# Talking-heads attention and a gated MLP on one core: score blocks, key transposes, mixing weights and low parts in another order

## The chip, the cores and the metric

The kernel runs on 1 core of one Trainium2 chip. The metric is the device time of one execution in microseconds, as the median of several runs. A profile of one further execution shows where the time goes. The engines are TensorE (PE in the rows, PEld for its weight loads), VectorE (DVE), ScalarE (ACT), GpSimd (POOL) and SyncE (SP), which only issues transfers.

## What is computed

Attention over 4 batches, 12 heads, 448 positions and 64 columns per head, in which the heads are mixed twice, and a two-layer MLP behind it:

```python
scores = scale * np.matmul(q, k.transpose(0, 1, 3, 2))
scores = np.einsum('bhij,hg->bgij', scores, w_pre)
scores = scores - np.max(scores, axis=-1, keepdims=True)
attn = np.exp(scores)
attn = attn / (np.sum(attn, axis=-1, keepdims=True) + 1e-09)
attn = np.einsum('bhij,hg->bgij', attn, w_post)
out = np.matmul(attn, v)
h = x @ w_in                      # x: out as 1792 x 768; w_in 768 x 2048, w_out 2048 x 768
y = (h * (1.0 / (1.0 + np.exp(-h)))) @ w_out
```

## The kernel before

The attention stage takes the first half of the span, the MLP the second. Query rows are cut into tiles of 120, 120, 120 and 100 rows for each batch; `seq` numbers these tiles n = 0 to 15. A tile is cut into groups of 10 query rows, so that it has 12, 12, 12 and 10 groups, and one pass of the loop over groups is a slot: slots 0 to 11 are tile 0, 36 to 45 tile 3 (the short one), and slot 46 begins batch 1 with tile 4. `first[n]` is the slot in which tile n begins.

For each tile, `prep_q` transposes q on TensorE (`pt`, ScalarE takes the high part `qh`, VectorE the low part `ql`), `prep_k` does the same for a pair of heads of the keys (`kh`, `kl`), once per batch. `scores` multiplies them for one pair of heads (`pqk`, six products in two PSUM banks); the even head is copied to `st` by ScalarE (L313), the odd one by VectorE (L311), and each copy is sent by SP to a tile `g` (L320), in which the rows lie as (query row, head). Head 11's rows go in two transfers of 5 partitions. `mix_pair` mixes the heads of two groups with `w_pre` (`pp`, L364), `top` takes the maxima (L370), `exp` the exponentials, `norm` the reciprocal and the scaled `w_post` (`wr`, on GpSimd), `mix_again` mixes with `w_post` (`pa`, L390), `put` evacuates it (L399), and `values` multiplies with v (`po`, L336). Beside this, `convert` turns the MLP's weights from 64-bit to 32-bit floats and writes them to DRAM: it loads `cw` and stores `wi_dram` by SP's queue and works a step per slot on VectorE, ScalarE and GpSimd.

What stands in which slot is written as a table: `put(i, what, ...)` files a step under slot i, and with `lead` a load so many slots sooner. The scores of tile n are filed in three blocks of two pairs of heads around the slots p0 = first[n - 1] of the tile before:

```python
i = p0 + ((-6, -2, 2) if n > 1 else (0, 0, 2))[h // 4]
for hg, i in ((0, p0 - 8), (1, p0 - 4)):            # prep_q, loads 4 slots sooner
for h, i, lead in zip(range(0, H, 2), (-5, -1, 3, 7, 11, 12), (4, 5, 4, 5, 5, 4)):   # keys, from c0 = first[n - 2]
```

A slot of the loop runs in this order: loads, `mix_pair` for the pair of groups LEAD = 4 slots ahead (even slots only), evacuations that earlier slots left, `top` of the fresh pair, the low parts and odd score copies that earlier slots left (VectorE), `norm`, `exp`, the steps filed for this slot, `mix_again`, a step of `convert`. The four banks of `ps_m` serve `pqk`, `pt` and `po`; the keys have two load buffers, the score copies six.

Ahead of the loop stands the start, written out by hand as `steps`: q and keys of batch 0, all scores of tile 0 and half of those of tile 1. `load_weights` is a generator that loads `w_pre` and `w_post` into `wrep` (memset L198; transfers L200 and L203 by GpSimd, L205 and L207 by SP), makes two masks, and builds `wpre` and `wpost` on VectorE (L220 to L225). Its parts are called at three places of the start. The two halves of tile 0's `g` are cleared by VectorE (L472).

Of the kernel before, what the change touches and what calls it, by code (L numbers as in the profile page):

```python
# [103 lines left out]
def talking_heads_then_silu_mlp(  # L104
# [11 lines left out]
    nc = tc.nc  # L116
    ctx.enter_context(tc.manual_schedule())
    B, H, S, D = q.shape
# [3 lines left out]
    RH = R // 2  # L122
    GP = 128
    HP = GP // 2
    GH = RH * H
    HS = H + 1
# [63 lines left out]
    def bank(p, name):  # L190
        return p.tile([128, 512], F32, name=name, tag="bank")

    g_tiles = [p.tile([GP, 12, S], F32, name="g", tag="g") for p in g_ps]

    def load_weights():

        wrep = e_p.tile([GP, 2, H], F32, name="wrep", tag="wr")
        nc.gpsimd.memset(wrep, 0.0)  # L198
        for r in (0, HP):
            nc.gpsimd.dma_start(  # L200
                out=wrep[r:r + GH, 1], in_=w_post.rearrange("h (o g) -> o h g", o=1).to_broadcast([RH, H, H]))
        for i in range(RH):
            nc.gpsimd.dma_start(out=wrep[HP + HS * i + 1:HP + HS * i + H, 0], in_=w_pre[:H - 1])  # L203
        yield
        nc.sync.dma_start(out=wrep[HP:HP + HS * (RH - 1) + 1:HS, 0], in_=w_pre[H - 1:].to_broadcast([RH, H]))  # L205
        for i in range(RH):
            nc.sync.dma_start(out=wrep[HS * i:HS * i + H, 0], in_=w_pre)  # L207
        yield
        def mask(rows, value):
            m = e_p.tile([GP, RH, 2], F32, name="mask", tag="wr")  # L210
            nc.gpsimd.memset(m, value)
            for sign in (1, -1):
                nc.gpsimd.affine_select(
                    out=m, in_=m, pattern=[[-rows * sign, RH], [-HP * sign, 2]], compare_op=ALU.is_ge, fill=0.0,
                    base=0 if sign > 0 else H - 1, channel_multiplier=sign)
            return m

        pre, blk = mask(HS, SCALE), mask(H, 1.0)
        one = e_p.tile([GP, RH, 1], F32, name="one", tag="wr")
        nc.vector.memset(wpre, 0.0)  # L220
        nc.vector.tensor_add(out=one, in0=pre[:, :, 0:1], in1=pre[:, :, 1:2])
        nc.vector.tensor_mul(
            out=wpre[:, :GH].rearrange("p (i g) -> p i g", i=RH), in0=one.to_broadcast([GP, RH, H]),
            in1=wrep[:, 0:1, :].to_broadcast([GP, RH, H]))
        nc.vector.tensor_mul(  # L225
            out=wpost, in0=wrep[:, 1, :].rearrange("p (g o) -> p g o", o=1).to_broadcast([GP, H, R]),
            in1=blk.rearrange("p (o i) s -> p o (i s)", o=1).to_broadcast([GP, H, R]))
# [35 lines left out]
    def load_q(n, hg, queue=nc.sync):  # L263
        b, ti = seq[n]
        t0, m, _ = tiles[ti]
        qns[n, hg] = nat.tile([TQ, HH, D], F32, name="qn", tag="qn", bufs=2)
        queue.dma_start(out=qns[n, hg][:m], in_=q[b, hg * HH:(hg + 1) * HH, t0:t0 + m, :].rearrange("h p d -> p h d"))
# [77 lines left out]
    class Group:  # L345
# [48 lines left out]
        def put(self):  # L394
            if self.slot == 0:
                ats[self.n] = a_p.tile([JT, NJ, H, TQ], F32, name="at", tag="at")
            o, np, p = self.place()
            o += (2 * p + self.slot % 2) * R
            nc.scalar.copy(out=ats[self.n].rearrange("p j g t -> p (j g) t")[:, :, o:o + R], in_=self.src)  # L399
# [17 lines left out]
    work = [[] for _ in range(len(groups) + 1)]  # L417
# [9 lines left out]
    for n in range(1, len(seq)):  # L427
        p0, p1 = first[n - 1], first[n]
        for h in range(0 if n > 1 else 2 * NE, H, 2):
            i = p0 + ((-6, -2, 2) if n > 1 else (0, 0, 2))[h // 4]  # L430
            put(i, scores, n, h, w=2.0)
            weight[i + 1] += 0.6
        if n > 1:
            for h, i in zip((0, HH), (p0 + 4, p0 + 8) if p1 - p0 == 12 else (p0 + 6, p0 + 9)):
                put(i, values, n - 2, h, w=0.6)
    for h, i in ((0, 4), (HH, 8)):
        put(first[-2] + i, values, len(seq) - 2, h, w=0.6)
    for n, (b, ti) in enumerate(seq):
        if n:
            p0 = first[n - 1]  # L440
            for hg, i in ((0, p0 - 8), (1, p0 - 4)):
                if n > 1:
                    put(i, load_q, n, hg, lead=4)
                if n > 1:
                    put(i, prep_q, n, hg, w=1.5)
            if ti == 0:
                c0 = first[n - 2]
                for h, i, lead in zip(range(0, H, 2), (-5, -1, 3, 7, 11, 12), (4, 5, 4, 5, 5, 4)):
                    put(c0 + i, load_k_pair, b, h, lead=lead)
                    put(c0 + i, prep_k, b, h, w=1.9)  # L450
        if ti == 0:
            for h in range(0, H, 2):
                i = first[n] + ((4, 6, 9, 11, 13, 15) if n else (1, 3, 5, 7, 9, 11))[h // 2]
                put(i, load_v_pair, b, h, lead=3)
# [7 lines left out]
    def keep_busy(n):  # L462
        p = bank(ps_a, "busy")
        for _ in range(n):
            nc.tensor.matmul(p[:, :128], lhsT=ident, rhs=ident, start=True, stop=True)

    keep_busy(7)
    first_scores = a_p.tile([TQ, H, S], F32, name="first", tag="at")
    weights = load_weights()
    next(weights)  # L470
    for w in (slice(0, 6), slice(6, 12)):
        nc.vector.memset(g_tiles[1][:, w], 0.0)  # L472
    load_q(0, 0)
    for h in range(0, 6, 2):
        load_k_pair(0, h, (nc.sync, nc.scalar))
# [9 lines left out]
            steps.append((prep_q, 0, 1))  # L485
    steps += [(prep_q, 1, 0)] + [(scores, 1, 2 * h) for h in range(2)] + [(prep_q, 1, 1)]
    steps += [(scores, 1, 2 * h) for h in range(2, NE)]
    next(weights)
    second = []
    for j, (what, *args) in enumerate(steps):  # L490
        banks[:] = [(ps_m, ps_m, ps_p, ps_a)[j % 4]]
        takes = what(*args)
        for take in (x for t in takes for x in t):
            if take:
                take()
        if j == 3:
            for _ in weights:
                pass
            load_q(1, 0, nc.gpsimd)
        if j == 5:  # L500
            load_q(1, 1, nc.gpsimd)
            for w in (slice(0, 6), slice(6, 12)):
                nc.gpsimd.memset(g_tiles[0][:, w], 0.0)
        if (what, *args) == (scores, 0, H - 2):
            for put_scores in second:
                put_scores()
    banks[:] = [ps_m]
    keep_busy(2)
    for i in range(0, LEAD, 2):
        at(i).mix_pair(at(i + 1), (ps_p, ps_m)[i // 2])  # L510
# [26 lines left out]
    for j in range(WB, len(parts)):  # L537
        kind, m = ("i", "o")[j // (7 * NP)], j // NP % 7
        kind0, m0, p0 = ("i", "o")[(j - WB) // (7 * NP)], (j - WB) // NP % 7, (j - WB) % NP
        n = HC if kind0 == "i" else HF  # L540
# [70 lines left out]
    later, done, scaled = [], [], False  # L611

    for i in range(len(groups) + 1):
# [26 lines left out]
        for take, _ in later:  # L640
            if take:
                take()
        if i < n_last:
            for x in fresh:
                x.top()
# [10 lines left out]
        later, done, highs = [], [], []  # L656
# [40 lines left out]
    later = [x for x in later + done]  # L697
    ready_part(len(ready))
    for h in (0, HH):
# [7 lines left out]
        later = [new]  # L707
# [154 lines left out]
```

## Time and profile before

| | before |
|---|---|
| median of 3 runs | 918.67 us (918.48 to 920.11) |
| profiled execution | 919.74 us, span 918.0 us |
| TensorE busy | 878.7 us (96% of the span), mean granted clock 0.981 |
| VectorE, ScalarE, GpSimd busy | 645.3, 536.5, 470.6 us |
| attention ends, about | 460 us |

The span is the time from the first to the last instruction; the rest of an execution's time lies around it. A busy share says little where the engines take turns: what matters is when TensorE stands, and what it waits for. Rows of a timeline give the start and the length in us, the engine, the source line, the operation and its tiles; in brackets stands how long the engine was idle before, and what released it. A granted clock of 1.00 is the full 2.4 GHz and 0.50 is 1.2 GHz. For SP, a row is the time in which it issued a transfer, not the transfer's own.

### The profile page before, as it was taken

To read this page: it belongs to the slowest core of one execution; us is meant where nothing else is said; L and a number is where in the kernel's file an instruction comes from. 1 tells how busy PE (TensorE), PEld (TensorE's weight loads), DVE (VectorE), ACT (ScalarE), POOL (GpSimd) and SP (SyncE) were. 2 spreads that over 40 slices of the span, in tenths; PEclk is the share of its full clock that TensorE was granted. 3 is DMA by queue.
4 is the path that set the end of the run, shared out by engine and by line. 5 is a ranking of instruction groups with operands and counts; after the bars stand their busy time and mean duration, and the time that the engine had idled before them with its cause. 6 is when DMAs were issued, how large, how long until landed. Compare 5 with 4: busy or idle time off the path is not lost.

```text
span 918.0 us, 19271 instructions
## 1 busy us (share of the span) xinstructions
PE 878.7 (96%) x6642; PEld 722.7 (79%) x6642; DVE 645.3 (70%) x1431; ACT 536.5 (58%) x1270; POOL 470.6 (51%) x648
## 2 busy tenths in 40 slices
PE   7699989999899999899999999999999999999997
PEld 5467757777577676677779998899999998989996
DVE  6578876888767788587631799955489958996242
ACT  4577776777767688487764555222476435434252
POOL 6145654555535455355522668993118737884030
PEclk8899999999989999999999999999999999999999
DMA  7688875888768877588600444122211232122134
GB/s 149 187 222 237 230 216 170 246 245 235 222 171 233 235 228 214 169 245 253 202 5 13 137 155 153 43 79 69 61 43 36 69 87 75 38 70 69 44 99 108
DMA packets 162161, 132.22 MB, mean 144 GB/s; under 512 B 50268, under 2 KB 155710, under 8 KB 162064
## 3 DMA queue, kind: packets, MB, share of 16 engines
q1 hardware_dynamic: 160032, 129.62, 49.3%
q0 software_dynamic: 640, 1.03, 0.5%
q8 instruction: 53, 0.87, 0.4%
q10 hardware_dynamic: 1392, 0.34, 0.2%
q14 instruction: 44, 0.36, 0.1%
HBM read 63.86 MB, written 27.53 MB: 100 GB/s over the span
## 4 chain that ended last, share of the span: by engine, by line
PE 74%; DMA 9%; DVE 9%; POOL 3%; issue 2%; ACT 1%; SPq 1%; POOLq 0%; DVEq 0%; ACTq 0%
PE pa L390 14%; PE ph L570 11%; PE ph L569 11%; PE ph L568 11%; PE pp L364 9%; PE po L336 9%; PE pqk L306 5%; DMA cw<-in_moe_w_in 3%; DMA g<-st 2%; DMA cw<-in_moe_w_out 2%; DVE nm L370 1%; PE pt L277 1%; POOL wl L558 1%; DVE op L576 1%; PE ptt L784 1%
## 5 line engine op out<-in xcount | busy, mean ns | idle before, releaser
L558 POOL TENSOR_TENSOR wl<-wl,wh 128x512 fp32r<-128x512 f32 x84 | 121.5, 1457 | 157.3 <-ACT wh L557 146.2
L383 POOL TENSOR_SCALAR wr<-wpost,r 128x120 f32<-128x120 f32 x184 | 87.1, 475 | 216.2 <-DVE r L381 136.9
L390 PEld LDWEIGHTS pa<-wr,e 128*112 128x112 f32 x1472 | 160.3, 178 | 24.9 <-issue 11.2
L390 PE MATMUL pa<-wr,e 128*112 128x120 f32 x1472 | 176.7, 272 | 0.0
L570 PE MATMUL ph<-op,wl 128*128 128x448 f32 x462 | 169.9, 368 | 2.6 <-POOL wl L558 2.6
L568 PE MATMUL ph<-op,wh 128*128 128x448 f32 x462 | 170.9, 370 | 0.0
L569 PE MATMUL ph<-op,wh 128*128 128x448 f32 x462 | 169.5, 367 | 0.0
L375 ACT ACTIVATE e<-pp,nm 128x448 f32<-128x448 f32 x184 | 116.7, 635 | 60.8 <-DVE nm L370 60.6
L370 DVE TENSOR_REDUCE nm<-pp 128x1 f32<-128x448 f32 x184 | 106.2, 619 | 52.7 <-PE pp L364 50.3
L364 PE MATMUL pp<-g,wpre 64*64 64x448 f32 x736 | 109.9, 582 | 16.1 <-DMA g<-st 9.0
L399 ACT COPY at<-pa 112x480 f32<-112x480 f32 x184 | 102.4, 589 | 6.8 <-PE pa L390 6.8
L336 PEld LDWEIGHTS po<-at,v 112*64 112x64 f32 x1536 | 79.5, 142 | 21.2 <-issue 14.1
L570 PEld LDWEIGHTS ph<-op,wl 128*128 128x128 f32 x462 | 86.8, 188 | 11.8 <-POOL wl L558 4.2
L568 PEld LDWEIGHTS ph<-op,wh 128*128 128x128 f32 x462 | 86.8, 188 | 7.5
L569 PEld LDWEIGHTS ph<-op,wh 128*128 128x128 f32 x462 | 86.9, 188 | 7.3
L66 POOL TENSOR_TENSOR cg<-cw,cg 128x256 f32<-128x256 f32 x96 | 73.1, 762 | 26.4 <-DVE cw L63 24.8
L336 PE MATMUL po<-at,v 112*64 112x120 f32 (+1 forms) x1536 | 86.4, 272 | 0.0
L557 ACT CAST wh<-wl 128x512 fp32r<-128x512 f32 x84 | 50.9, 618 | 48.8 <-DMA wl<-wo_dram 23.6
L576 DVE TENSOR_TENSOR op<-x,op 128x448 fp32r<-128x448 f32 x54 | 46.5, 871 | 34.5 <-ACT op L574 19.7
L90 ACT ACTIVATE cg<-cg,ebias 128x256 int32<-128x256 int32 x96 | 50.8, 529 | 24.6 <-DVE cg L86 16.2
L364 PEld LDWEIGHTS pp<-g,wpre 64*64 64x64 f32 x736 | 25.5, 135 | 39.3 <-issue 18.6
L311 DVE COPY st<-pqk 120x448 f32<-120x448 f32 (+1 forms) x90 | 51.9, 611 | 5.1 <-DMA g<-st 2.0
(114 smaller groups left out, 1602.7 us busy)
## 6 DMA issues: line engine op xcount, KB each, us to landing
g<-st SPq DMA_DIRECT2D x121, 210.0 KB
cw<-in_moe_w_in SPq DMA_DIRECT2D x48, 256.0 KB
cw<-in_moe_w_out SPq DMA_DIRECT2D x48, 256.0 KB
wi_dram<-cg SPq DMA_DIRECT2D x24, 448.0 KB
wo_dram<-cg SPq DMA_DIRECT2D x24, 448.0 KB
wl<-wi_dram SPq DMA_DIRECT2D x42, 256.0 KB
wl<-wo_dram SPq DMA_DIRECT2D x42, 256.0 KB
g<-st SPq DMA_DIRECT2D x44, 175.0 KB
```

Source lines behind the costliest of these rows:

```text
L66: nc.gpsimd.tensor_mul(out=e, in0=m, in1=e)
L336: nc.tensor.matmul(po[i * D:(i + 1) * D, c * m:(c + 1) * m], lhsT=vs[b, h + 2 * c][:, i, j, :], rhs=ats[n][:, j, h + 2 * c + i, :m], start ...
L364: nc.tensor.matmul((self, other)[r].p[HP * c:HP * (c + 1), :S], lhsT=wpre[rows], rhs=gs[self.n][rows, o // R + c * np + p, :], start=True, ...
L370: nc.vector.tensor_reduce(out=self.nm, in_=self.p[:GP, :S], axis=AX.X, op=ALU.max, negate=True)
L375: nc.scalar.activation(out=self.e, in_=self.p[:GP, :S], func=AF.Exp, bias=self.nm, scale=1.0, accum_out=self.s)
L383: nc.gpsimd.tensor_scalar(out=self.wr, in0=wpost.rearrange("p g i -> p (g i)"), scalar1=r, scalar2=1.0, op0=ALU.mult, op1=ALU.mult)
L390: nc.tensor.matmul(self.pa[:JT, j * H * R:(j + 1) * H * R], lhsT=self.e[:, j * JT:(j + 1) * JT], rhs=self.wr, start=True, stop=True)
L399: nc.scalar.copy(out=ats[self.n].rearrange("p j g t -> p (j g) t")[:, :, o:o + R], in_=self.src)
L558: nc.gpsimd.tensor_sub(out=wl, in0=raw(wl), in1=raw(wh))
L568: nc.tensor.matmul(p[:, :T], lhsT=wh, rhs=x[:, 0], start=(n == 0), stop=False)
L569: nc.tensor.matmul(p[:, :T], lhsT=wh, rhs=x[:, 1], start=False, stop=False)
L570: nc.tensor.matmul(p[:, :T], lhsT=wl, rhs=x[:, 0], start=False, stop=(n == nk - 1))
```

## The change

It has five parts. (1) The last score block of a tile whose predecessor has ten slots is filed at p0 + 1 instead of p0 + 2: slots 37, 83 and 129 instead of 38, 84 and 130. (2) The key transposes of the next batch's last two pairs are filed at c0 + 8 and c0 + 11 instead of c0 + 11 and c0 + 12, with leads 4 and 3. (3) All loads of `wrep` go by GpSimd's queue, and `wpre` and `wpost` are built behind step 10 of the start instead of step 3; the second half of tile 0's `g` is cleared by GpSimd. (4) The first half of q of tile 2 is loaded by GpSimd's queue ahead of the loop instead of by SP in slot 0. (5) In a slot with scores, low parts and score copies left by earlier slots are taken ahead of the maxima.

```diff
@@ load_weights
         for i in range(RH):
             nc.gpsimd.dma_start(out=wrep[HP + HS * i + 1:HP + HS * i + H, 0], in_=w_pre[:H - 1])
-        yield
-        nc.sync.dma_start(out=wrep[HP:HP + HS * (RH - 1) + 1:HS, 0], in_=w_pre[H - 1:].to_broadcast([RH, H]))
-        for i in range(RH):
-            nc.sync.dma_start(out=wrep[HS * i:HS * i + H, 0], in_=w_pre)
-        yield
+            nc.gpsimd.dma_start(out=wrep[HS * i:HS * i + H, 0], in_=w_pre)
+        nc.gpsimd.dma_start(out=wrep[HP:HP + HS * (RH - 1) + 1:HS, 0], in_=w_pre[H - 1:].to_broadcast([RH, H]))
...
         one = e_p.tile([GP, RH, 1], F32, name="one", tag="wr")
+        yield
         nc.vector.memset(wpre, 0.0)
@@ the table
-            i = p0 + ((-6, -2, 2) if n > 1 else (0, 0, 2))[h // 4]
+            i = p0 + ((-6, -2, 2 if p1 - p0 == 12 else 1) if n > 1 else (0, 0, 2))[h // 4]
...
-                if n > 1:
+                if n > 1 and (n, hg) != (2, 0):
                     put(i, load_q, n, hg, lead=4)
...
-                for h, i, lead in zip(range(0, H, 2), (-5, -1, 3, 7, 11, 12), (4, 5, 4, 5, 5, 4)):
+                for h, i, lead in zip(range(0, H, 2), (-5, -1, 3, 7, 8, 11), (4, 5, 4, 5, 4, 3)):
@@ the start
-    for w in (slice(0, 6), slice(6, 12)):
-        nc.vector.memset(g_tiles[1][:, w], 0.0)
+    for eng, w in ((nc.vector, slice(0, 6)), (nc.gpsimd, slice(6, 12))):
+        eng.memset(g_tiles[1][:, w], 0.0)
...
-    next(weights)
     second = []
...
         if j == 3:
-            for _ in weights:
-                pass
             load_q(1, 0, nc.gpsimd)
...
+        if j == 10:
+            for _ in weights:
+                pass
...
     banks[:] = [ps_m]
+    load_q(2, 0, nc.gpsimd)
@@ the loop over slots
+        if any(what is scores for what, _ in work[i]):
+            for _, take in later:
+                if take:
+                    take()
+            later = []
         if i < n_last:
             for x in fresh:
                 x.top()
```

TensorE's rows at the first border, before, from slot 36's key transposes to slot 40's mix: `pt<-ident,kn` are key transposes, `pp` the mix, `pa` the second mix, `pqk` the scores of tile 4's last block.

```order
L247 MATMUL pt<-ident,kn 128x112 x4
L390 MATMUL pa<-wr,e 112x120 x8
L364 MATMUL pp<-g,wpre 64x448 x4
L306 MATMUL pqk<-kh,qh 120x448 x2
L306 MATMUL pqk<-kh,ql 120x448 x2
L306 MATMUL pqk<-kl,qh 120x448 x2
L306 MATMUL pqk<-kh,qh 120x448 x2
L306 MATMUL pqk<-kh,ql 120x448 x2
L306 MATMUL pqk<-kl,qh 120x448 x2
L277 MATMUL pt<-ident,qn 128x120 x3
L390 MATMUL pa<-wr,e 112x120 x8
L364 MATMUL pp<-g,wpre 64x448 x4
```

TensorE's rows at the same place after the change, from slot 36's mix to slot 38's second mixes:

```order
L362 MATMUL pp<-g,wpre 64x448 x4
L388 MATMUL pa<-wr,e 112x120 x4
L304 MATMUL pqk<-kh,qh 120x448 x2
L304 MATMUL pqk<-kh,ql 120x448 x2
L304 MATMUL pqk<-kl,qh 120x448 x2
L304 MATMUL pqk<-kh,qh 120x448 x2
L304 MATMUL pqk<-kh,ql 120x448 x2
L304 MATMUL pqk<-kl,qh 120x448 x2
L388 MATMUL pa<-wr,e 112x120 x4
L362 MATMUL pp<-g,wpre 64x448 x4
L275 MATMUL pt<-ident,qn 128x120 x3
L388 MATMUL pa<-wr,e 112x120 x8
```

The score products stand ahead of the mix of slot 38 instead of behind it, and q's transposes no longer follow them in the same slot; the key transposes of slot 36 are gone from here.

SP's queue at the same place, before; `g_131<-st` are the score stores of tile 4's last block (heads 8, 10, 9 and 11, the last in two transfers):

```order
L47 DMA cw_1838<-in_moe_w_in 128x2x256
L47 DMA cw_1900<-in_moe_w_in 128x2x256
L57 DMA wi_dram_67<-cg_1664 128x896
L267 DMA qn_1906<-in_q 120x6x64
L320 DMA g_131<-st_1944 10x12x448
L320 DMA g_131<-st_1965 10x12x448
L320 DMA g_131<-st_1968 10x12x448
L320 DMA g_131<-st_1971 5x12x448 x2
L47 DMA cw_1986<-in_moe_w_in 128x2x256
```

And after the change:

```order
L47 DMA cw_1847<-in_moe_w_in 128x2x256
L318 DMA g_131<-st_1911 10x12x448
L47 DMA cw_1919<-in_moe_w_in 128x2x256
L57 DMA wi_dram_67<-cg_1664 128x896
L265 DMA qn_1925<-in_q 120x6x64
L318 DMA g_131<-st_1934 10x12x448
L318 DMA g_131<-st_1941 10x12x448
L318 DMA g_131<-st_1944 5x12x448 x2
L47 DMA cw_1986<-in_moe_w_in 128x2x256
```

Head 8's store has moved ahead of a `cw` load, the `wi_dram` store and a q load; the stores of heads 10, 9 and 11 still stand behind these three.

VectorE's rows at the start, before: `kl` and `ql` are low parts, `first` the score copies of tile 0, `wpre` and `wpost` the weights that the mixes need.

```order
L290 TENSOR_TENSOR ql<-pt,qh 128x3x3x20 x2
L255 TENSOR_TENSOR kl<-pt,kh 128x448 x3
L220 MEMSET wpre 128x64
L221 TENSOR_TENSOR one<-mask 128x5
L222 TENSOR_TENSOR wpre<-one,wrep 128x60
L225 TENSOR_TENSOR wpost<-wrep,mask 128x120
L311 COPY first<-pqk 120x448
L290 TENSOR_TENSOR ql<-pt,qh 128x3x3x20 x2
L255 TENSOR_TENSOR kl<-pt,kh 128x448
L311 COPY first<-pqk 120x448
```

And after the change, from the first three key splits on:

```order
L253 TENSOR_TENSOR kl<-pt,kh 128x448 x3
L309 COPY first<-pqk 120x448
L288 TENSOR_TENSOR ql<-pt,qh 128x3x3x20 x2
L253 TENSOR_TENSOR kl<-pt,kh 128x448
L309 COPY first<-pqk 120x448
L253 TENSOR_TENSOR kl<-pt,kh 128x448
L309 COPY first<-pqk 120x448
L253 TENSOR_TENSOR kl<-pt,kh 128x448
L218 MEMSET wpre 128x64
L219 TENSOR_TENSOR one<-mask 128x5
L220 TENSOR_TENSOR wpre<-one,wrep 128x60
L223 TENSOR_TENSOR wpost<-wrep,mask 128x120
```

The four rows that build the weights have moved behind the last key split, past three score copies, and ahead of the last three.

## Rows read from the trace of the kernel before

**Rows 1.** The windows by stretch: us, then each engine's busy us, granted clock, DMA

```profile
133.10:143.40 10.30, 6.93 (x58) 4.23 (x57) 3.31 (x11) 1.92 (x5) 1.67 (x3) 0.67 0.75 224
247.30:258.20 10.90, 7.50 (x56) 5.21 (x56) 3.44 (x11) 1.89 (x5) 3.38 (x7) 0.69 0.82 245
366.10:376.00 9.90, 5.88 (x57) 3.60 (x56) 3.26 (x11) 1.93 (x5) 1.68 (x3) 0.83 0.76 231
...
460.00:918.00 458.00, 449.18 (x2424) 408.03 (x2423) 303.26 (x418) 211.78 (x425) 239.33 (x198) 1.00 0.25 73
```

**Rows 2.** TensorE's waits before 470 us: total us, times, longest us

```profile
PE pp L364 <- DMA g<-st: 9.0, 8, 3.4
PE pt L277 <- DMA qn<-in_q: 5.6, 3, 3.9
...
PE pt L277 <- ACT st L313: 2.9, 3, 1.0
```

**Rows 3.** The timeline, TensorE before and at the first border: start us, us

```profile
110.54 2.68 PE L336 MATMUL po<-at,v 112*64 112x120 f32 x48
...
119.78 0.98 PE L364 MATMUL pp<-g,wpre 64*64 64x448 f32 x8
...
126.78 0.53 PE L277 MATMUL pt<-ident,qn 120*128 120x120 f32 x3 [1.03 <-ACT st L313]
...
136.48 3.22 PE L364 MATMUL pp<-g,wpre 64*64 64x448 f32 x8 [3.37 <-DMA g<-st]
...
139.62 3.81 PE L336 MATMUL po<-at,v 112*64 112x120 f32 x48
```

**Rows 4.** The timeline, SP's queue, VectorE and ScalarE ahead of that border

```profile
112.76 1.79 SPq L234 DMA_DIRECT2D kn<-in_k  x2
...
122.30 1.06 SPq L47 DMA_DIRECT2D cw<-in_moe_w_in  x2
...
123.44 1.05 SPq L57 DMA_DIRECT2D wi_dram<-cg  x1
...
124.59 0.39 SPq L267 DMA_DIRECT2D qn<-in_q  x1
...
126.75 6.10 SPq L320 DMA_DIRECT2D g<-st  x5
...
126.90 1.14 DVE L311 COPY st<-pqk 120x448 f32<-120x448 f32 x2
...
129.00 0.55 ACT L313 COPY st<-pqk 120x448 f32<-120x448 f32 x1
```

**Rows 5.** The timeline of the start, all engines

```profile
3.11 2.54 POOL L203 DMA_DIRECT2D wrep<-in_w_pre  x5
...
4.28 2.30 DVE L472 MEMSET g<- 128x2688 f32 x1 [0.51 <-issue]
...
9.86 0.53 ACT L313 COPY first<-pqk 120x448 f32<-120x448 f32 x1 [0.65 <-PE pqk L306]
...
12.74 18.26 SPq L320 DMA_DIRECT2D g<-first  x20
...
14.08 0.22 DVE L222 TENSOR_TENSOR wpre<-one,wrep 128x60 f32<-128x60 f32 x1 [4.11 <-DMA wrep<-in_w_pre]
...
15.09 0.46 PE L306 MATMUL pqk<-kh,qh 64*120 64x448 f32 x1 [1.53 <-DVE first L311]
...
28.60 4.73 PE L364 MATMUL pp<-g,wpre 64*64 64x448 f32 x24 [3.16 <-DMA g<-first]
```

**Rows 6.** The timeline, the two q loads of tile 2

```profile
44.91 0.86 PE L277 MATMUL pt<-ident,qn 120*128 120x120 f32 x3 [3.88 <-DMA qn<-in_q]
...
48.41 0.33 SPq L267 DMA_DIRECT2D qn<-in_q  x1
...
57.20 0.53 PE L277 MATMUL pt<-ident,qn 120*128 120x120 f32 x3 [1.19 <-DMA qn<-in_q]
```

**Rows 7.** DMA issues: KB each, median us from issue to landing

```profile
wrep<-in_w_pre POOLq DMA_DIRECT2D x5, 0.5 KB, 5.1
```

## Prediction

> **What bounds the kernel now.** I read the windows by stretch first. From 460 us to the end TensorE is busy 449 of 458 us at full clock, and no edit touches that stage [rows 1]. What TensorE loses lies before: at the start, and at three short places near 133, 247 and 366 us, which last 10.3, 10.9 and 9.9 us with TensorE busy 6.93, 7.50 and 5.88 us at a mean granted clock of 0.67, 0.69 and 0.83 [rows 1]. The list of waits names the causes before 470 us: score stores that have not landed in g (9.0 us in 8 waits), q loads (5.6 us in 3), and score copies that still hold a PSUM bank (2.9 us in 3) [rows 2]. So a step here is worth what it takes from these waits, with the half clock behind them, until the next late thing shows.
>
> **One border, read in order of time.** Groups are mixed in pairs four slots ahead, so tile 4's first pair (slots 46, 47) is mixed in slot 42, and all its score rows must be in g by then. Its last score block stands in slot 38. There TensorE first waits 1.03 us for a bank (four score products and the q transposes want five, ps_m has four); 9.7 us later its first mix of tile 4 waits 3.37 us for the stores [rows 3]. Why are they late? Head 10's copy on ScalarE starts only at 129.00. VectorE's copies were done at 128.04, but their stores stand behind head 10's in SP's queue, so five stores hold SP from 126.75 to 132.85 [rows 4]. The mix starts 136.48 - 132.85 = 3.6 us later; that is the landing. After the wait this mix takes 3.22 instead of 0.98 us and the 48 value products 3.81 instead of 2.68 [rows 3].
>
> The price of all three borders: each window holds 0.98 + 2.68 = 3.66 us of work at full clock. Window minus work is 6.6, 7.2 and 6.2 us; of these 3.4, 3.4 and 4.0 are idle (length minus busy), and 3.3, 3.8 and 2.2 are half clock. With the bank waits of 2.9 the borders cost 23 us.
>
> **Edits 1 and 2, score block and key transposes.** The block moves from slot 38 to 37 (and the same at the two later borders), the key transposes of pairs 8 and 10 from slots 35, 36 to 32, 35. TensorE's work stays the same in sum; four transposes of a key pair (about 0.6 us, as the three of q take 0.53 [rows 3]) go ahead of the slot-36 mix, which I put at 120.4 instead of 119.78. With the durations of the rows the score products then run from 122.2 to 123.6, the mix of slot 38 until 125.5, and TensorE reaches slot 42 at about 131.7: 133.11, where its wait begins now, less the 1.03 for the bank, which no longer lacks, and 0.4 of small gaps.
>
> The stores, in SP's new order: head 8's copy comes after slot 37's exponential and evacuation, about 124.4. Then a cw load, a wi_dram store and a q load go first (0.53 + 1.05 + 0.39 [rows 4]), so head 10's store starts about 127.0, though its copy is ready at 125.7. Heads 9 and 11 gain little at their source: slot 38 is even, so their copies stand behind two maxima that wait for its mix. At 0.57 us each [rows 4] two maxima and two copies end at 127.8, against 128.04 before. Four stores from 127.0 at 0.84 us (below) end at 130.4, against 132.85. With the same 3.6 us of landing that is 134.0: **2.4 us sooner, and still a wait of 2.3 us instead of 3.37 + 1.03.** Bounds: if only its own copy held head 10, the stores end at 129 and land at 132.6; if the three transfers ahead hold the rings, nothing comes sooner. Half clock is the open part. Behind waits of 3.16, 3.37 and 3.88 us the next products were slow (24 mixing products took 4.73 us, q's transposes 0.86), behind 1.19 us they were not (0.53) [rows 3, 5, 6]. At 2.3, between these, I count half of the mean 3.1 us as saved. Per border 2.4 + 1.6 = 4.0; **three borders 12 us**, bounds 0 and 23.
>
> Edit 2 has one price: pair 10's keys are still loaded in slot 32, but used a slot sooner. SP issues them at 112.76 [rows 4], their transposes come at 119.1: a lead of 6.3 us. Counted at nothing, as a load that lands within that; one q load in the crowded start took 8.8 [rows 6].
>
> **Edit 3, the weights.** Before, VectorE stands 4.11 us until 14.08 for weights that SP issues behind the key loads. Behind this wait, in order, stands the copy of head 1, whose product was ready with head 0's, by 9.86; TensorE then stands 1.53 us for the bank, and SP's second store goes out only behind that copy, at about 15.06 [rows 5]. After the edit VectorE meets the weights behind its last key split, near 15 us. Eleven w_pre loads of 0.51 us from 3.11 on, the later ones held by an earlier one's 5.1 us of landing, are issued by about 10 and land by 15 [rows 5, 7]. SP sends 20 stores in 18.26 us with that hole of some 1.5 in it, so 0.84 us each. Thirteen must land before the first mix. Now the first goes at 12.74 and twelve from 15.06, which ends at 25.1. From 10.4, when head 0's copy is done [rows 5], and never starved, thirteen end at 21.3. **First mix 3.8 us sooner**, bounds 2 (heads 10 and 11 come late) and 5. The half memset of 2.30 us that goes from VectorE to GpSimd [rows 5] delays tile 1's two q loads there to about 18.8 and 20.3, when their transposes are due: at nothing, or 1 us if late.
>
> Here a rule speaks against the edit. The rows show w_pre loads on GpSimd's queue at 0.51 us each, some of them beside a VectorE memset of 2.30 us [rows 5]. The Trainium skill, SBUF — State Buffer, section "A bandwidth-pool intuition that's wrong (but worth ruling out)", says that a transfer issued by GpSimd waits for its descriptors while VectorE holds their common port, and tells of one that went from about 620 to 3100 ns. By the rows the loads are issued by 10; what such a hold would make of the sum is rival E.
>
> **Edit 4, q of tile 2.** Its first half is now issued by GpSimd before the loop. That takes away the 3.88 us wait at 44.91 and the slow products behind it [rows 6]. But SP sends stores without a pause to 31 us and is hardly free up to 46; next late is the other q half, issued at 48.41 and waited for until 57.20 [rows 6]. By then only what SP's chain gained counts: the 3.8 us, 0.4 of issue, part of the clock. I take 5.5 us for edits 3 and 4 together, bounds 2 and 10.
>
> **Edit 5, low parts ahead of maxima.** It acts only in a slot with scores whose predecessor left parts pending. Scores stand in even slots and in 37, 83 and 129, and the slots before them hold no work. So it moves nothing: 0.
>
> **Sum**, on the profiled execution: 919.74 (span 918.0 and 1.74 around it) - 5.5 - 12 = 902.2. That execution lies 1.07 us over the median 918.67; I forecast 902.
>
> **Rivals.** *B, the wait hardly moves:* head 10 stays behind three transfers that fill the rings, half clock stays, and the start's gain is lost to the next late load. 1.5 per border, 3 at the start: 912 (908 to 916). For it: SP's new order. *C, no wait left:* landing by 132, no half clock; 6.6 per border and 6.5 at the start: 919.7 - 26.3 = 893 (886 to 897). For it: the tiles between the borders run the same block six slots ahead and put no long wait in the list [rows 2]. *D, keys late:* pair 10's keys land after their transposes. It decides from 6.3 us on; at 8.8 us the score products come 2.5 us after 122.2, past their old place, and the borders gain nothing: 919.7 - 5.5 = 914. Against it: no key load in the list of long waits. *E, slower:* each of the eleven w_pre loads is held by a VectorE operation. Held 0.57 us each, by a copy, they land 6 us later and the first mix 1 us later than now. Held 2.30 us each, as by a memset, they are issued by 28 and land near 33; heads 7, 9 and 11, behind the wait, then cost SP four more stores and a landing, 33 + 3.4 + 3.6 = 40, 11.4 us later than now, and the q loads behind them 3 more: 919.7 + 14.4 - 12 = 922. It is slower than before once the weights land after 31 us. Against it: the 0.51 us.
>
> **Chances:** forecast 0.50 (896 to 908), B 0.20, C 0.20, D 0.05, E 0.03, none of these 0.02. The range 888 to 914 leaves out E and the ends of B and C. About 0.2% is what a measurement tells from no change: faster than that 0.93, within it 0.03, slower 0.04.
>
> **What would show it.** Right: the first mix near 24.8 us; VectorE without its wait of 4 us; no q wait in slot 4; three waits of about 2 us for g in place of 3 to 4; no bank wait before q's transposes. Wrong: border waits of 3 us or more, or none; key transposes that wait; VectorE waiting for the weights; a q wait of 6 us in slot 8 that takes the start back.

## The result and the profile after

The changed kernel takes 908.49 us (median of 4 runs, 908.17 to 909.73) against 918.58 us for the kernel before on the same chip (4 runs, 916.64 to 920.11): ratio 0.9894, interval 0.9873 to 0.9915. That is 10.1 us less, where 16.7 was forecast. 908.5 lies within the range (888 to 914), and the sign is right. It lies just outside the band of the forecast itself (896 to 908) and in that of rival B (908 to 916), and the gain is not made up as the prediction said. One of the six runs of a kernel below (only pair 8 moved) took 1065 us at a granted clock of 0.75 and is left out of that kernel's median and ratio.

Stretches of the changed kernel, from TensorE's arrival at tile 4's, 8's and 12's first mix to the end of the value products behind it, and the MLP; the last row is that stage in the kernel before. The columns are the window, its length, the busy us (and instructions) of TensorE, of its weight loads, of VectorE, ScalarE and GpSimd, the granted clock, the DMA engines' busy share, and GB/s.

```profile
136.48:143.00 6.52, 4.52 (x57) 2.94 (x58) 3.63 (x12) 2.54 (x7) 2.54 (x6) 1.00 0.71 207
249.01:254.68 5.67, 4.13 (x57) 2.94 (x58) 3.54 (x12) 2.51 (x7) 3.40 (x7) 1.00 0.72 236
361.39:367.56 6.17, 4.52 (x58) 2.94 (x58) 3.61 (x12) 2.53 (x7) 2.52 (x6) 1.00 0.61 177
467.58:906.50 438.92, 430.14 (x2273) 395.84 (x2272) 292.90 (x388) 199.56 (x393) 236.45 (x189) 1.00 0.26 76
```

```profile
476.07:918.00 441.93, 433.11 (x2273) 395.99 (x2272) 294.50 (x388) 199.49 (x393) 234.53 (x189) 1.00 0.26 75
```

The borders fell from 10.3, 10.9 and 9.9 us [rows 1] to 6.5, 5.7 and 6.2, at full clock. The MLP, which no edit touches, took 441.9 us in the one execution profiled before and 438.9 in this one. In twelve of the thirteen executions profiled of the change and of the kernels below it took 438.7 to 439.8, so 3 of the 11.5 us between the two spans belong to that execution, not to the change. The medians are free of this.

TensorE's waits before 470 us, changed kernel:

```profile
PE pp L362 <- ACT at L397: 4.4, 3, 1.5
PE pt L245 <- DMA kn<-in_k: 4.2, 5, 1.3
PE pp L362 <- DMA g<-first: 4.0, 1, 4.0
PE pp L362 <- DMA qn<-in_q: 3.5, 1, 3.5
PE pp L362 <- DMA g<-st: 2.4, 4, 0.8
...
PE pt L275 <- DMA qn<-in_q: 1.1, 2, 0.6
```

Beside [rows 2]: the waits for q in slot 4 (3.88 us) and for a bank (2.9 us) are gone, the waits for score rows at the borders are 1.5 to 2.0 us each (the first row holds the larger part; it names ScalarE's copies to `at`, which the mix neither reads nor overwrites, while at two of the three borders its next products wait once more for `g`, so I take it to be the rows). New are waits for keys at the borders (three of the five; the other two are at the start), and a wait of 3.5 us ahead of slot 8's mix, put down to q, which the mix does not read, and so again a wait for score rows.

The first border in order of time, TensorE and SP's queue:

```profile
122.42 0.57 PE L245 MATMUL pt<-ident,kn 112*128 112x112 f32 x4 [0.49 <-DMA kn<-in_k]
...
127.75 0.79 SPq L318 DMA_DIRECT2D g<-st  x1
...
128.65 0.44 SPq L47 DMA_DIRECT2D cw<-in_moe_w_in  x1
...
129.18 0.41 SPq L57 DMA_DIRECT2D wi_dram<-cg  x1
...
129.68 0.53 SPq L265 DMA_DIRECT2D qn<-in_q  x1
...
130.30 4.41 SPq L318 DMA_DIRECT2D g<-st  x4
...
137.99 0.93 PE L362 MATMUL pp<-g,wpre 64*64 64x448 f32 x2 [1.51 <-ACT at L397]
...
139.42 0.98 PE L362 MATMUL pp<-g,wpre 64*64 64x448 f32 x6 [0.49 <-DMA g<-st]
...
140.32 2.68 PE L334 MATMUL po<-at,v 112*64 112x120 f32 x48
```

Head 10's store stands behind three transfers, as forecast, and four stores end at 134.7. The value products take 2.68 us instead of 3.81 [rows 3]: full clock. Pair 10's keys come late, by 0.49 us here and 1.24 and 0.54 at the other borders.

The start, changed kernel: a window with the columns of the first fence; then SP's stores and TensorE's mixes.

```profile
8.00:20.00 12.00, 11.71 (x58) 8.01 (x58) 7.60 (x18) 6.02 (x13) 7.99 (x14) 0.57 0.58 124
```

```profile
11.27 20.52 SPq L318 DMA_DIRECT2D g<-first  x20
...
29.00 3.32 PE L362 MATMUL pp<-g,wpre 64*64 64x448 f32 x16 [4.01 <-DMA g<-first]
...
54.00 0.93 PE L362 MATMUL pp<-g,wpre 64*64 64x448 f32 x2 [3.48 <-DMA qn<-in_q]
...
55.77 1.77 PE L362 MATMUL pp<-g,wpre 64*64 64x448 f32 x6 [0.84 <-DMA g<-st]
```

The first mix stands at 29.00 us, where 24.8 was forecast and 28.60 measured before [rows 5], and by the value products of slot 28 (103.27 us, 100.39 before) this execution was 2.9 us behind the one before. From that came the first theory of the runs: all the gain comes from the borders, the start loses.

### The profile page after: what moved, and what is told of

It is laid out like the page before. It is cut to its first block, busy times and chain, and to the rows that moved or that the text cites. A ratio compares the mean times of both kernels' runs of the same rounds, so it can differ in the third digit from the quotient of the medians.

```text
span 906.5 us, 19265 instructions
## 1 busy us (share of the span) xinstructions
PE 873.7 (96%) x6642; PEld 720.2 (79%) x6642; DVE 640.3 (71%) x1430; ACT 536.9 (59%) x1270; POOL 478.0 (53%) x656
## 4 chain that ended last, share of the span: by engine, by line
PE 73%; DMA 9%; DVE 9%; POOL 4%; issue 3%; ACT 2%; SPq 1%; POOLq 0%; ACTq 0%; DVEq 0%
PE pa L388 14%; PE ph L569 12%; PE ph L568 11%; PE ph L567 11%; PE pp L362 8%; PE po L334 8%; PE pqk L304 5%; DMA g<-st 3%; DMA kn<-in_k 2%; DMA qn<-in_q 2%; PE pt L275 1%; POOL wl L557 1%; DVE op L575 1%; PE pt L245 1%; PE ptt L788 1%
## 5 line engine op out<-in xcount | busy, mean ns | idle before, releaser
L334 PEld LDWEIGHTS po<-at,v 112*64 112x64 f32 x1536 | 75.5, 137 | 19.1 <-issue 12.7
L334 PE MATMUL po<-at,v 112*64 112x120 f32 (+1 forms) x1536 | 82.4, 264 | 0.0
L362 PEld LDWEIGHTS pp<-g,wpre 64*64 64x64 f32 x736 | 25.8, 134 | 38.9 <-issue 11.5
```

The lines of the kernel that those rows point to most:

```text
L334: nc.tensor.matmul(po[i * D:(i + 1) * D, c * m:(c + 1) * m], lhsT=vs[b, h + 2 * c][:, i, j, :], rhs=ats[n][:, j, h + 2 * c + i, :m], start ...
L362: nc.tensor.matmul((self, other)[r].p[HP * c:HP * (c + 1), :S], lhsT=wpre[rows], rhs=gs[self.n][rows, o // R + c * np + p, :], start=True, ...
```

## Experiments

Each run gives a median beside the kernel before on the same chip; chips differ between the three groups of four, so kernels of different groups are compared by their ratios. "us" behind a ratio is that share of the kernel before. The ratio is taken from all the runs and lies up to 0.003 (2.6 us) from the quotient of the two medians; where the two tell a different story, both are given.

### The parts one at a time

The block alone:

```diff
-            i = p0 + ((-6, -2, 2) if n > 1 else (0, 0, 2))[h // 4]
+            i = p0 + ((-6, -2, 2 if p1 - p0 == 12 else 1) if n > 1 else (0, 0, 2))[h // 4]
```

> The kernel before with the score block moved alone (slots 37, 83, 129 for 38, 84, 130); key transposes and the start as before. Theory 1 (ledger of the two traces: the three borders gave 10.5 us, of which TensorE's waits for keys at the borders, 0.49 + 1.24 + 0.54 = 2.3 us, took something back, and these come from the moved key transposes): the block alone gives the whole border gain without those waits, 12 to 13 us, so about 906, with the start as before (first mix near 28.6 us, q wait of 3.9 us in slot 4). Rival (the moved key transposes are needed, since with pair 10's keys in slot 36 their high and low parts come late for slot 37's products): a wait of 1 us or more ahead of slot 37's products at each border, and 6 to 9 us gained, 910 to 913.

Block and key transposes (the same, and this):

```diff
-                for h, i, lead in zip(range(0, H, 2), (-5, -1, 3, 7, 11, 12), (4, 5, 4, 5, 5, 4)):
+                for h, i, lead in zip(range(0, H, 2), (-5, -1, 3, 7, 8, 11), (4, 5, 4, 5, 4, 3)):
```

> The kernel before with the score block and the key transposes moved; the start as before. Theory 1: the borders give 10.5 us and the start is not spoiled: 908 (907 to 909), as fast as the whole change or 1 to 3 us faster. Rival (the start's edits do help and the MLP's pace hides it): 912 to 914.

The weights alone (all w_pre loads on GpSimd, weights built behind step 10, half of the clearing on GpSimd):

```diff
-        for i in range(RH):
-            nc.sync.dma_start(out=wrep[HS * i:HS * i + H, 0], in_=w_pre)
+            nc.gpsimd.dma_start(out=wrep[HS * i:HS * i + H, 0], in_=w_pre)
...
+        if j == 10:
+            for _ in weights:
+                pass
```

> The kernel before with the weights' loads on GpSimd's queue, the building of the weights moved, and half of the clearing on GpSimd; all else as before. Theory 1: the first mix stays at 28.5 to 29 us, since SP's stores of tile 0 are paced by TensorE's score products at half clock and not by VectorE's wait: 918.6 to 920, no change or 1 us slower. Rival (the prediction's): the first mix 3.8 us sooner, 24.8 us, and 2 to 4 us gained, 915 to 917.

The q load alone:

```diff
-                if n > 1:
+                if n > 1 and (n, hg) != (2, 0):
                     put(i, load_q, n, hg, lead=4)
...
+    load_q(2, 0, nc.gpsimd)
     keep_busy(2)
```

> The kernel before with the first half of tile 2's q loaded by GpSimd ahead of the loop; all else as before. Theory 1: the q wait of 3.9 us in slot 4 goes, but TensorE then waits 3 to 4 us for tile 1's score rows in slot 8, which DMA rings busy at 0.95 and more deliver no sooner, and a stretch of half clock follows: 918 to 921, nothing gained or 2 us lost. Rival (the prediction's): 3 to 4 us gained, 915.

| kernel | median us (before 918.65) | ratio | interval |
|---|---|---|---|
| block | 906.18 | 0.9882 | 0.9859 to 0.9905 |
| block and keys | 910.25 | 0.9919 | 0.9899 to 0.9940 |
| weights | 916.25 | 0.9981 | 0.9962 to 0.9999 |
| q load | 918.01 | 0.9993 | 0.9973 to 1.0012 |

By the ratios the block alone gives 10.8 us, where the whole change gave 9.7 (the intervals overlap); with the moved keys only 7.4 is left. The weights give 1.7 us, in an interval that ends just short of no gain, which speaks against the theory of a start that loses; the q load gives nothing that can be told from zero. TensorE's waits from 20 to 470 us with the block alone:

```profile
PE pt L277 <- DMA qn<-in_q: 8.8, 4, 5.3
PE pqk L306 <- DVE r L380: 3.2, 4, 1.0
PE pp L364 <- DMA g<-first: 2.4, 1, 2.4
PE pp L364 <- DMA g<-st: 1.6, 4, 0.5
```

No key wait; per border one wait of 0.8 to 1.0 us in slot 37 (second row, three of the four), which ends when VectorE has taken pair 10's low part out of its bank, and 0.3 to 0.9 us at the mix. With the weights alone the first mix is 2.75 us sooner than in the profile before. SP, TensorE and GpSimd there:

```profile
9.93 18.83 SPq L318 DMA_DIRECT2D g<-first  x20
...
13.91 0.93 POOL L265 DMA_DIRECT2D qn<-in_q  x1
...
18.00 0.53 PE L275 MATMUL pt<-ident,qn 120*128 120x120 f32 x3 [2.43 <-DMA qn<-in_q]
...
18.31 0.87 POOL L265 DMA_DIRECT2D qn<-in_q  x1 [2.87 <-issue]
...
24.70 1.22 PE L463 MATMUL busy<-ident 128*128 128x128 f32 x4
25.85 2.12 PE L362 MATMUL pp<-g,wpre 64*64 64x448 f32 x16
```

No wait stands ahead of this mix: TensorE comes to it straight from its idle products (L463), after it has waited 2.43 us for the first half of tile 1's q. The rows had landed by then. GpSimd issues that q load at 13.91 us; in the kernel before at 7.48 us:

```profile
7.48 0.93 POOL L267 DMA_DIRECT2D qn<-in_q  x1 [0.53 <-PE pt L247]
```

### Back to the old key place, a longer lead, later v loads

The second group: the changed kernel again; the same with the key transposes and leads of before; the same as changed, but with pair 6's transposes in slot 30 and pair 10's keys loaded in slot 31; and the second of these with batch 0's v loads later.

> The changed kernel once more, as the one to compare the next three with, and for a second look at its start. Theory 1 (the first four runs: block alone -10.8 us at the median, key transposes +3.4, weights -1.7, q load 0): 908.5 again, with a first mix between 25.8 and 29 us, as executions of one start differ by 1.5 us. Rival (the whole change's start is slower than that of its parts, as the one profile with its half clock from 8 to 18 us showed): a first mix at 28.5 us or later again.

```diff
-                for h, i, lead in zip(range(0, H, 2), (-5, -1, 3, 7, 8, 11), (4, 5, 4, 5, 4, 3)):
+                for h, i, lead in zip(range(0, H, 2), (-5, -1, 3, 7, 11, 12), (4, 5, 4, 5, 5, 4)):
```

> The changed kernel with the key transposes back at slots 35 and 36 and their old leads. Theory 1 (moved key transposes cost 3.4 us, at every border TensorE waits 1.3 to 1.7 us for keys loaded three slots sooner): 905 (904 to 906.5), faster than both kernels, no key wait at the borders. Rival (block and start do not add up, since what the start gains is lost to the next late transfer): 908, as the whole change.

```diff
-                for h, i, lead in zip(range(0, H, 2), (-5, -1, 3, 7, 8, 11), (4, 5, 4, 5, 4, 3)):
+                for h, i, lead in zip(range(0, H, 2), (-5, -1, 3, 6, 8, 11), (4, 5, 4, 4, 4, 4)):
```

> The changed kernel with pair 6's transposes a slot sooner (30) and pair 10's keys loaded in slot 31 instead of 32, so that the lead of pair 10 is four slots; its transposes stay in slot 35, where the change put them. Theory 1 (the cost of the moved key transposes is the short lead): no key wait at the borders, and 904 to 905.5, as with the old place or a little faster, as the wait for pair 10's low part of about 1 us per border, which the block alone has, is gone as well. Rival (the cost is the place of the transposes): 908, as the whole change, with waits elsewhere.

```diff
-                i = first[n] + ((4, 6, 9, 11, 13, 15) if n else (1, 3, 5, 7, 9, 11))[h // 2]
+                i = first[n] + ((4, 6, 9, 11, 13, 15) if n else (10, 11, 12, 14, 15, 16))[h // 2]
```

> As the changed kernel with the key transposes at their old place, and the six loads of batch 0's v moved from slots 0 to 8 to slots 7 to 13. Theory 1 (between 32 and 54 us the rings are the bound: about 3.8 MB are issued there, some 17 us at the 225 GB/s of those windows, so tile 1's score rows land late for slot 8's mix whatever is done about q): 0.67 MB less ahead of them, 3 us; the wait in slot 8 falls from 4.3 us to 1 to 2 us, and the kernel is 2 to 3.5 us faster than the one without it. Rival (SP's own time for issuing the stores, or the score copies, bound it): the wait stays above 3 us and less than 1 us is gained.

| kernel | median us (before 917.51) | ratio | interval |
|---|---|---|---|
| changed, again | 908.57 | 0.9906 | 0.9878 to 0.9934 |
| old key place | 904.98 | 0.9855 | 0.9832 to 0.9878 |
| longer lead | 912.53 | 0.9947 | 0.9924 to 0.9970 |
| old key place, v later | 901.45 | 0.9827 | 0.9801 to 0.9852 |

The second execution of the changed kernel had its first mix at 25.26 us instead of 29.00, again without a wait ahead of it. The old key place is 3.6 us faster than the change. **The longer lead refutes my account of why**: its key waits are gone, yet it is 4.0 us slower than the change. TensorE's waits from 20 to 470 us, longer lead:

```profile
PE pp L362 <- DMA v<-in_v: 5.8, 1, 5.8
PE pp L362 <- DMA g<-st: 5.3, 4, 3.3
PE pp L362 <- ACT cg L90: 2.1, 1, 2.1
...
PE pt L245 <- ACT st L311: 1.7, 3, 0.6
PE pp L362 <- ACT at L397: 1.6, 1, 1.6
```

At the borders the mixes now wait 3.3, 2.1 and 2.0 us for score rows, and pair 6's transposes wait 0.56 us for a bank at each (the row of L245).

The later v loads bring 3.5 us more by the medians (2.6 by the ratios, whose intervals overlap). Windows from 40 to 60 us, without and with them, and slot 8's mix in both:

```profile
40.00:60.00 20.00, 13.60 (x83) 8.07 (x76) 11.38 (x34) 10.17 (x25) 5.75 (x12) 0.83 0.86 217
```

```profile
53.38 3.17 PE L362 MATMUL pp<-g,wpre 64*64 64x448 f32 x8 [4.08 <-DMA cw<-in_moe_w_in]
```

```profile
40.00:60.00 20.00, 18.48 (x142) 12.44 (x142) 16.71 (x52) 14.70 (x36) 8.27 (x17) 1.00 0.86 237
```

```profile
48.28 0.93 PE L362 MATMUL pp<-g,wpre 64*64 64x448 f32 x2
...
49.38 0.98 PE L362 MATMUL pp<-g,wpre 64*64 64x448 f32 x6 [0.17 <-DMA g<-st]
```

The wait of 4.08 us in slot 8 is gone, with the slow mix behind it (3.17 us for eight products that take 0.98 at full clock). This kernel is faster than the change and than the kernel before by more than its interval.

### What the keys cost, and what the start gives

The third group: block and later v loads without the edits of the start; the change with only pair 8's transposes moved; the change with pair 8's in slot 34; and three more idle products in the start of the fastest kernel.

> The kernel before with the score block and the later v loads, and without the edits of the start (weights and q of tile 2 as before). Theory 1 (the rings between 32 and 54 us took back what the edits of the start gave; with 0.67 MB out of the way their gain shows): 906 to 907, 4.5 to 5.5 us slower than the same kernel with them (901.5), with a q wait of 3 to 5 us in slot 4. Rival (the edits of the start are worth 2.5 us in any case, as without the later v loads): 904. Second rival (the later v loads do the work of the q edit too, since the q load of slot 0 no longer stands behind two v loads): 902.

```diff
-                for h, i, lead in zip(range(0, H, 2), (-5, -1, 3, 7, 8, 11), (4, 5, 4, 5, 4, 3)):
+                for h, i, lead in zip(range(0, H, 2), (-5, -1, 3, 7, 8, 12), (4, 5, 4, 5, 4, 4)):
```

> The changed kernel with pair 10's keys back at slot 36 and only pair 8's in the new place (slot 32, lead 4). Theory 1 (what costs 3.6 us is pair 10's move: its keys are late, or, where they are not, TensorE comes to tile 4's mix before the rows have landed): 905, no key wait at the borders, waits of 0.4 to 0.7 us ahead of the first mix of tile 4. Rival (pair 8's transposes in slot 32, beside tile 3's other work, cost it): 908.5, with mix waits of 1.5 us or more.

```diff
-                for h, i, lead in zip(range(0, H, 2), (-5, -1, 3, 7, 8, 11), (4, 5, 4, 5, 4, 3)):
+                for h, i, lead in zip(range(0, H, 2), (-5, -1, 3, 7, 10, 11), (4, 5, 4, 5, 4, 3)):
```

> The changed kernel with pair 8's transposes in slot 34 instead of 32 and pair 10's in slot 35 as in the change, lead 3. Theory 1 (pair 10's move costs): 908.5 or more, key waits of 0.5 to 1.5 us at the borders and mix waits of 1 us and more. Rival (pair 8's move costs): 905 to 906.

```diff
+        if j in (0, 2):
+            keep_busy(2 - j // 2)
```

> The fastest kernel so far (block, start's edits, old key transposes, later v loads; 901.5) with three more idle products of TensorE between q's and the first keys' transposes, where it waits 0.55 to 1.25 us and then 0.7 to 0.9 for keys. Theory 1 (granted clocks of 0.5 to 0.6 between 8 and 16 us stand behind these waits in some executions and not in others, and cost the first mix 1 to 3 us in them): the clock stays at 1.00 until 20 us, the first mix stands at 26 us or sooner, and the median falls by 0.5 to 1.5 us. Rival (the clock at the start is set by something else, or SP's stores hide it): 901.5, or half a microsecond slower for the products themselves.

| kernel | median us (before 920.23) | ratio | interval |
|---|---|---|---|
| block, v later, old start | 907.58 | 0.9891 | 0.9858 to 0.9923 |
| only pair 8 moved | 909.28 | 0.9896 | 0.9862 to 0.9930 |
| pair 8 in 34, pair 10 in 35 | 910.67 | 0.9911 | 0.9879 to 0.9942 |
| fastest, more idle products | 903.44 | 0.9840 | 0.9810 to 0.9869 |

Without the start's edits the later v loads give nothing that can be told from zero (0.9891 against 0.9882 for the block alone). With the later v loads the start's edits are worth 0.0064, 5.9 us (0.9827 against 0.9891, whose intervals do not meet; within this group 907.58 - 903.44 = 4.1 us); without them 0.0027, 2.5 us (0.9855 against 0.9882, whose intervals do overlap). By the quotients of the medians the two figures are 3.5 and 0.1 us. In both counts the edits of the start are worth some 3.4 us more with the later v loads than without, but that difference is smaller than the intervals of the four ratios together, so it is likely, but not shown.

Both key variants are by the ratios about as slow as the change (the interval with only pair 8 moved still meets that of the old place, 0.9832 to 0.9878), so pair 10's move is not what costs alone, as I had thought. With only pair 8 moved no key waits at a border, but the mixes wait 2.1, 2.5 and 1.2 us for rows. With pair 8 in slot 34 and pair 10 in 35 the two key transposes wait 0.57 and 1.31 us for a bank at every border, and the mixes 1.4 to 2.6.

The idle products gained nothing that shows. The test says little: the clock was 1.00 from 8 to 20 us with them, but in the profiled execution without them too.

## Why the prediction was right or wrong

**The border term: 12 us was forecast for edits 1 and 2 together. The block alone gave about that; the two together did not, because edit 2, counted at nothing, took a third of it back.** To see the borders alone, take the time from the start of slot 28's value products to those of slot 45 (100.39 to 148.79 us before), and the same at the other two borders, and add the three. In the kernel before it is 145.4 us; 142.1 and 143.6 with the weights and the q load alone, so 143.7 in mean. In the five kernels with the block and the old key place it is 131.5 to 132.4, in mean 131.9: **11.8 us, where 12 was forecast**. With moved keys, in six executions, it is 134.8 to 142.0, in mean 138.8: 4.9 us.

That 11.8 meets 12 is in part luck. The forecast had per border a wait of 2.3 us for rows, no bank wait, and half of the slow stretch kept. With the old key place the waits at the mix are 0.3 to 0.9 us, the clock never falls, and a wait of 0.8 to 1.0 us for a bank stands in slot 37, which the prediction did not have. The price was also a little high: it took 3.66 us of work for the mix and the value products of a border, and the changed kernel's windows are busy 4.1 to 4.5 us at full clock for the same products.

In the changed kernel itself the steps held one by one: no bank wait before q's transposes; the wait for rows 1.5 to 2.0 us, not 2.3; four stores issued behind `cw`, `wi_dram` and q; and the half clock partly saved. The two executions of the change differ in just that. Windows of 16 us from shortly before the wait at the third border, first and second execution:

```profile
359.00:375.00 16.00, 14.35 (x165) 10.93 (x163) 11.70 (x36) 10.36 (x28) 8.92 (x18) 1.00 0.56 177
```

```profile
360.00:376.00 16.00, 13.93 (x117) 10.13 (x117) 8.45 (x25) 8.24 (x23) 6.25 (x13) 0.79 0.44 135
```

Behind waits of 1.65 and 2.06 us the clock stayed at 1.00 in the first, and fell to 0.79 in mean in the second, whose border took 3.4 us longer. Over all kernels: at the fifteen borders with the old key place the clock stayed at 1.00 throughout; at the eighteen with moved keys it fell at eight, behind waits of 1.9 to 3.3 us at the mix, and not at the other ten, where those waits were 2.1 us or less. Where the clock falls a border loses most of its gain (3.4 us there, of some 3.9).

Edit 2 was priced by pair 10's lead alone, "Counted at nothing, as a load that lands within that". By the medians it cost 4.1 us beside the block and 3.6 in the whole change. The key waits of 0.49, 1.24 and 0.54 us were real, which is rival D's mechanism at a smaller size, but are not what decides: three variants without them were about as slow or slower. What the moved places share is longer waits at the mix: 0.8 to 3.3 us at 17 of 18 borders, instead of 0.3 to 0.9 at all 15 with the old place, at six of which the profile names ScalarE's exponentials and not the rows. SP had issued the last of these stores 8.9 to 9.2 us after the block's first product with the old place, 7.7 to 9.4 with the moved ones; the last part of the mix began 3.2 to 4.7 us after that with the old place, and 3.7 to 5.9 in those 17. Part of the wait is plain: in the old place TensorE stands 0.8 to 1.0 us for a bank in slot 37, and comes to the mix later by that. (With only pair 8 moved it stands 0.3 to 0.6 us there.) Why the rows land later when key transposes ahead of the block are moved was not settled.

**The start: the term of 5.5 us was mis-sized, for three reasons.** The first is the rate of the stores: "From 10.4 [...] and never starved, thirteen end at 21.3" failed. With the edit stores began at 9.6 to 11.3 us, and VectorE's wait for weights is gone, but the twenty take 18.8 to 20.5 us instead of 18.26 [rows 5]: 0.94 to 1.03 us each rather than 0.84. In the first profile of the change TensorE's products ran at half clock from about 8 to 18 us, two copies came only every 2.3 to 2.9 us, and the first mix waited 4.01 us for these rows, until 29.00.

The second is a term that the prediction put "at nothing, or 1 us if late": tile 1's two q loads on GpSimd's queue. Behind the weights' loads and the memset they are issued at 13.1 to 14.0 and 17.8 to 18.7 us instead of 7.5 and 12.3 to 13.2, and in eight of the nine executions with this edit TensorE waits 0.8 to 3.3 us for them (not at all with the old start). In those eight nothing is waited for ahead of the first mix: it stands where TensorE arrives, at 25.3 to 28.4 us, and sooner rows would not have moved it. So with the weights alone the first mix came 2.75 us sooner than in the profile before, 1.3 to 2.8 sooner than in the five executions with the old start (27.1 to 28.7), and not 3.8. No run has these q loads ahead of the weights' loads.

The third: what the start gains is handed to the next late thing. The prediction named it, but as a q wait in slot 8. It was tile 1's score rows there, 4.3 us in the change and 4.8 in its second execution, while the q wait itself fell to 0.5 us and less. With the q load alone 2.2 and 0.8 us stand there for rows, and nothing was gained. (The q wait of slot 4 does not show it: 5.02 us with the weights alone, 3.9 to 5.3 with the old start and the v loads in place.) What stands ahead of these rows shows in SP's queue, old key place without and with the later v loads (the last `g` rows are tile 1's last stores):

```profile
37.62 1.00 SPq L236 DMA_DIRECT2D v<-in_v  x2
38.72 1.65 SPq L318 DMA_DIRECT2D g<-st  x2
40.42 0.53 SPq L236 DMA_DIRECT2D v<-in_v  x1
41.36 4.68 SPq L318 DMA_DIRECT2D g<-st  x5
```

```profile
36.81 6.29 SPq L318 DMA_DIRECT2D g<-st  x7
```

Three v loads stood ahead of them. With these moved the stores are out at 43.1 instead of 46.0 us, the wait goes, and the edits of the start are worth 5.9 us by the ratios (3.5 by the medians), where 5.5 was forecast without that move. The 3 us expected for 0.67 MB less came out at 2.6 to 3.5; how much of it is SP's time and how much that of the DMA engines the runs do not part. The rows fit what the Trainium skill, Trainium Kernel Development and Optimization, section "Key Constraints", says: transfers issued by SP, ScalarE and GpSimd run on the same DMA engines, and another issuer saves only the time to issue. With the q load on GpSimd tile 1's last stores were out at 46.0 us, and at 46.4 before.

**Rival E did not happen.** GpSimd issued each of the eleven w_pre loads in 0.50 to 0.54 us, the first two of them partly beside VectorE's memset; pauses of 0.33 to 0.76 us stood before three later ones, each ended by an earlier landing. The rule weighed in the prediction (the Trainium skill, SBUF — State Buffer, section "A bandwidth-pool intuition that's wrong (but worth ruling out)") does not show in these rows; with two loads beside a memset, and only in part, they test it little.

**Edit 5** moves nothing, as forecast: from 60 us on the traces of the change and of block and keys, which lacks it, have the same instructions in the same order on every engine.

**Rival B**, in whose band the median fell, had the start right and the border wrong: the start's gain was lost to the next late rows, but the wait for rows fell from 3.4 to 4.0 us to 1.5 to 2.0, and half clock stayed in only some executions.

So the sum, by the ratios: 10.8 for the block, less 3.4 for the keys, plus some 2.5 for the start makes 9.9, where 9.7 and 8.6 were measured (10.1 and 8.9 by the medians). Forecast were 12, 0 and 5.5. (The terms add to 17.5 and the forecast to 16.7, because the sum was taken from an execution 1.07 us above the median and rounded.) Both terms were too large, 12 against 7.4 and 5.5 against 2.5, and the range was wide enough for it.

## What to carry to other kernels

Price a step that is moved out of the way like any other: here the transposes that made room for the score block cost a third of its gain, and undoing them was worth 3.6 us. Where one queue feeds several deadlines, a load that is taken off a wait may pay only when the transfers around the next deadline are thinned as well: by the ratios the edits of the start gave 2.5 us alone and 5.9 with the v loads out of the way. Where loads are moved to another queue, look at what stood there already: here tile 1's q came late behind the weights. And one profile is one execution: it showed a start that lost 3 us where the medians showed a gain.

## What the runs showed of the hardware

The granted clock at the start differs from execution to execution of the same instructions. The kernel before, the block, block and keys, the q load, and block with later v loads have the same instructions up to 23 us; from 8 to 20 us their mean granted clocks were 0.72, 0.86, 0.72, 1.00 and 0.52, and their first mixes stood at 28.60, 28.39, 27.14, 27.48 and 28.68 us. The change itself had 0.57 and 0.72, with first mixes at 29.00 and 25.26.

The MLP stage took 438.7 to 439.8 us in twelve executions and 441.9 and 442.4 in two, at a granted clock of 1.00 and with TensorE busy in the same share; what slows it in those was not found.
